# A fused attention and mixture kernel on one Trainium2 core: token copies, the first exponential, three operand splits and the read-back of g are placed anew

## The chip, the core and the metric

The kernel runs on one core of a Trainium2 chip. The core has five instruction streams that wait for one another by semaphores: TensorE (PE in the rows; its weight loads are PEld), VectorE (DVE), ScalarE (ACT), GpSimd (POOL) and SyncE (SP), which here issues every DMA. The metric is the device time of one execution in microseconds, median of several runs. The profile is of one further execution.

## What is computed

The reference, cut to what matters (the shapes are B=4, H=12, S=448, D=64; 1792 tokens of width 768; 8 experts of 4 slots, width 1024):

```python
scores = q @ k.T / sqrt(64) - log(448)          # per batch and head
x      = sigmoid(scores) @ v                    # -> (1792, 768)
g      = (x @ w_a) * (x @ w_b)                  # (1792, 1536)
x2     = g @ w_out                              # (1792, 768)
logits = x2 @ phi                               # (1792, 32)
d      = exp(logits - max over tokens); d /= sum over tokens
slot_in  = d.T @ x2                             # 32 slots
slot_out = relu(slot_in @ w1[e]) @ w2[e]        # 4 slots for each of 8 experts
c      = exp(logits - max over slots);  c /= sum over slots
out    = c @ slot_out
```

w_a, w_b and w_out come as 8-byte floats and are turned into 4-byte ones on the chip.

## The kernel before, in words

**Splits.** Most products are made of three matmuls: an operand t is kept as a rounded part (name with h) and a rest t - h (name with l), and hi x hi, hi x lo and lo x hi are summed in PSUM. So every operand costs one cast and one subtraction. `split_x`, `late_operands` and `block` make them; `late_operands` casts on ScalarE and subtracts on VectorE or GpSimd, by the name of the operand.

**Attention.** The 48 heads go in 24 pairs g. For a pair, `emit_TK` and `emit_TQ` transpose k and q through the two "ms" banks of PSUM, `emit_S` makes the scores of one of four chunks c and ScalarE turns each into a sigmoid (L185), `emit_PV` multiplies by v (16 matmuls, L195) and `emit_x` copies the result out of its "sc" bank (L218; L222 for batch 0). `att()` is a generator that yields after each piece. From pair 12 on (and before pair 6) a pair is "dense": its first chunk and the next pair's transposes stand ahead of the PV of the pair before it, then chunks 1, 2 and 3 follow. There are four "sc" banks, two "ab" banks (chunk 2 uses them in dense pairs) and two "ms" banks.

**The stages.** (1) Pairs 0 to 5. (2) `ab(0)`: g for batch 0, with pairs 6 to 11 woven in and w_a, w_b converted (`beats`) and written to DRAM as `ab32`. (3) The loop over `att_g` with pairs 12 to 23; beside it `operands()` makes sums of batches 1 and 2 on GpSimd, `prep_u(0)` the first weight blocks, and the first softmax step runs as a filler. (4) Twelve `unit(u)`s: batches 1 and 2 are multiplied together by a seven-product scheme; product m of a unit takes the operands ORDER = A11, S2, A12, S3, S1, A22, S4 (nine groups: three matmuls each of hi x hi, lo x hi, hi x lo) and one weight block `block(u, m)`, which is a cast on ScalarE and a subtraction on GpSimd (L574). T2, T3 and T4 are weight differences that VectorE makes from the raw tile `wr` (L583 to L589). Unit u+1's blocks are prepared during unit u by stepping `pu`, one step per product. S3, S1, A22 and S4 are the "late" operands, made at the start of unit 0, in memory that attention frees after its last PV. (5) `ab(3)`: g for batch 3; its weights come one half-product ahead from `ab32` (`load_w`, L425, the tiles `wr`), are cast on VectorE and subtracted on GpSimd (`split`, L433, L434). (6) `last_LG`, the slots, the experts' w1 and w2 from a ring of tiles (`pump`), and the output.

**Fillers.** `fill` is a list of generators; `fill_step` runs one step of the first. `group(b, gi)` turns four finished g tiles into tokens by transposes and copies (L486, L488). `LG(b)` makes the logits of batch b (matmul L716 into an "ms" bank `lf`), the maximum (VectorE), the exponential d and a copy of the logits (ScalarE, L733 and L738), transposes both (`tokens`, L752) and adds d.T @ g to `acc` (`dg`, L761). ScalarE has to load another function table ahead of the exponential and again ahead of the next sigmoid.

**g of batches 1 and 2.** Four token tiles are written to DRAM as `gk32` during the units and read back in `reload_gk` at i == 6 of `ab(3)` (i counts its yields, six to a column of weights) for LG(1) and LG(2). `pump` then loads one tile of `out32` or of an expert into each open slot, at every third i.

**What sets the order.** Each engine runs its instructions in the order in which the code emits them; an instruction waits only for semaphores. SP too is in order: a DMA that waits holds up all that are issued behind it, and nothing else makes SP keep pace with the loop that emitted it.

## Time and profile before

| what | us |
|---|---|
| median of 3 runs | 717.5 (716.67 to 718.07) |
| the profiled execution's own time | 717.61 |
| its span in the trace | 715.6 |
| mean granted TensorE clock | 0.984 of full |
| pairs 12 to 23 (stage 3) | about 215 to 311 |
| start of unit 0 up to unit 1 | 311 to 335 |
| units to the end | up to 485 |
| ab(3) | 485 to 600 |
| last softmax step | 600 to 623 |
| experts and output | 623 to 715.6 |

The stages are read from the timeline; 0 is the span's start. The execution's time is 2.0 us longer than the span, and 0.1 us longer than the median. In a timeline row the columns are start, length, engine, line, operation, output<-input, shape and count; the brackets give the idle time of that engine ahead of the row and what ended it. Lengths of neighbouring matmul rows overlap a little at their ends, so distances are taken from start to start. The granted clock is a share of full speed: 1.00 is 2.4 GHz and 0.50 is 1.2 GHz.

### The profile page before, as it was taken

The numbers are of one execution on the slowest core, as the hardware profiler recorded it, in microseconds if no ns is written. First come the engines' busy times: TensorE is split into PE (matmuls) and PEld (weight loads), VectorE is DVE, ScalarE is ACT, GpSimd is POOL, SyncE is SP. The second block draws the span as 40 slices with busy tenths as digits, with TensorE's granted clock in tenths as the row PEclk, the third lists the DMA queues.
The fourth block names the chain that finished last, engine by engine and source line by source line (L and its number), as shares of the span: only waits on it lengthen the run. The fifth ranks groups of instructions, "written<-read, shape, count | busy, mean of one in ns | idle before, by whom it ended". The sixth has DMA issues, their size and how long they took to land.

```text
span 715.6 us, 11048 instructions
## 1 busy us (share of the span) xinstructions
PE 663.9 (93%) x4187; PEld 476.7 (67%) x4187; DVE 358.9 (50%) x520; ACT 307.9 (43%) x557; POOL 303.2 (42%) x232
## 2 busy tenths in 40 slices
PE   6999999999999899998999999999979999997683
PEld 4557877776775454556998998898868896432131
DVE  4666899889735235226775567644323222300022
ACT  4887777878735577664233323311201011100021
POOL 0243677666634048009985665652333542100000
PEclk9999999999999999999999999999989999999998
DMA  8998999999724233201113411430997986999998
GB/s 200 254 295 207 287 310 302 271 300 283 227 84 136 72 81 76 70 2 46 38 53 80 147 52 45 118 140 23 259 352 277 367 307 229 359 416 415 410 352 270
DMA packets 104819, 146.90 MB, mean 205 GB/s; under 512 B 50880, under 2 KB 83904, under 8 KB 100800
## 3 DMA queue, kind: packets, MB, share of 16 engines
q1 hardware_dynamic: 104768, 146.22, 63.5%
q8 instruction: 33, 0.54, 0.3%
q14 instruction: 18, 0.15, 0.1%
HBM read 122.69 MB, written 23.50 MB: 204 GB/s over the span
## 4 chain that ended last, share of the span: by engine, by line
PE 77%; DMA 11%; DVE 4%; ACT 3%; POOL 2%; issue 1%; SPq 1%; ACTq 0%; DVEq 0%; POOLq 0%
PE ab L518 23%; PE sc L684 13%; PE sc L195 10%; DMA e<-in_moe_w 9%; PE sc L182 7%; PE ab L684 7%; PE ms L149 3%; PE ms L486 2%; DMA wr<-ab 2%; PE ab L182 1%; PE ms L468 1%; PE ms L761 1%; PE ms L377 1%; PE ms L364 1%; DVE gk L334 1%
## 5 line engine op out<-in xcount | busy, mean ns | idle before, releaser
L339 POOL TENSOR_TENSOR w<-gk,cy 128x768 int32<-128x768 int32 x36 | 66.2, 1839 | 91.6 <-DVE gk L334 60.1
L185 ACT ACTIVATE a<-sc,sums 112x448 f32<-112x448 f32 x158 | 89.2, 645 | 16.6 <-PE sc L182 16.5
L195 PE MATMUL sc<-a,vn 112*64 112x448 f32 x384 | 78.9, 552 | 2.7 <-ACT a L185 2.7
L518 PE MATMUL ab<-t,wh 128*128 128x448 f32 x288 | 66.0, 375 | 4.3 <-DVE wh L433 4.3
L434 POOL TENSOR_TENSOR wl<-wr,wh 128x768 fp32r<-128x768 f32 x22 | 40.5, 1840 | 68.1 <-DVE wh L433 39.6
L518 PEld LDWEIGHTS ab<-t,wh 128*128 128x128 f32 x288 | 54.0, 191 | 9.1 <-DVE wh L433 4.4
L195 PEld LDWEIGHTS sc<-a,vn 112*64 112x64 f32 x384 | 26.0, 138 | 41.9 <-issue 35.0
L525 ACT COPY misc<-ab 128x448 f32<-128x448 f32 x24 | 12.8, 534 | 77.0 <-PE ab L518 77.0
L434 POOL TENSOR_TENSOR wl<-w,wh 128x768 fp32r<-128x768 f32 x24 | 44.3, 1846 | 2.5 <-ACT wh L433 2.5
L1063 PE MATMUL ab<-e,gk 128*32 128x384 f32 x240 | 32.9, 521 | 12.4 <-DMA e<-in_moe_w 12.4
L332 DVE TENSOR_SCALAR mf<-gk 128x768 f32<-128x768 f32 x36 | 34.1, 946 | 13.8 <-ACT gk L321 13.6
L182 PE MATMUL sc<-qh,kh 64*112 64x448 f32 x158 | 36.6, 427 | 2.4 <-ACT a L185 1.0
L333 DVE TENSOR_SCALAR gk<-mf 128x768 uint32<-128x768 uint32 x36 | 34.3, 953 | 1.2
L518 PE MATMUL ab<-xh,wh 128*128 128x448 f32 x144 | 34.9, 377 | 0.0
L574 POOL TENSOR_TENSOR wx<-wr,wx 128x384 fp32r<-128x384 f32 x29 | 33.7, 1165 | 2.3 <-ACT wx L573 2.1
L518 PE MATMUL ab<-xl,wh 128*128 128x448 f32 x144 | 34.5, 375 | 0.0
L518 PE MATMUL ab<-xh,wl 128*128 128x448 f32 x144 | 34.5, 375 | 0.0
L518 PE MATMUL ab<-t,wl 128*128 128x448 f32 x144 | 34.0, 371 | 0.0
L1063 PEld LDWEIGHTS ab<-e,gk 128*32 128x32 f32 x240 | 9.6, 114 | 34.7 <-DMA e<-in_moe_w 23.9
L528 DVE TENSOR_TENSOR misc<-misc,ab 128x448 f32<-128x448 f32 x24 | 14.8, 616 | 35.0 <-PE ab L518 35.0
L574 POOL TENSOR_TENSOR wx<-T,wx 128x384 fp32r<-128x384 f32 x23 | 24.0, 1042 | 18.3 <-ACT wx L573 18.3
L573 ACT CAST wx<-T 128x384 fp32r<-128x384 f32 x23 | 11.8, 512 | 46.3 <-DVE T L589 30.9
(423 smaller groups left out, 1472.9 us busy)
## 6 DMA issues: line engine op xcount, KB each, us to landing
e<-in_moe_w SPq DMA_DIRECT2D x23, 1024.0 KB, 7.1
e<-in_moe_w SPq DMA_DIRECT2D x23, 768.0 KB, 15.1
wr<-ab SPq DMA_DIRECT2D x14, 768.0 KB, 4.9
ab<-w SPq DMA_DIRECT2D x24, 384.0 KB, 7.1
wr<-ab SPq DMA_DIRECT2D x18, 384.0 KB, 4.6
kn<-in_k SPq DMA_DIRECT2D x48, 112.0 KB, 4.7
qn<-in_q SPq DMA_DIRECT2D x48, 112.0 KB, 3.9
vn<-in_v SPq DMA_DIRECT2D x24, 224.0 KB, 3.9
```

What stands on the lines that cost most here:

```text
L149: pe.transpose(t[:, c * T:(c + 1) * T], a[:, c].rearrange("p h d -> p (h d)"), ident[:T, :T])
L182: pe.matmul(sc[h], kx[r, cs], qx[r], start=(i == 0), stop=(i == 2))
L185: act.activation(a, sc[h], AF.Sigmoid, bias=nlog[:T], scale=1.0 / math.sqrt(D))
L195: pe.matmul(pv_t[g][64 * h:64 * h + 64], qkv_t["v", g][:, h, c, :], a_t.pop((g, h, c)), start=(c == 0), stop=(c == C - 1))
L332: dve.tensor_scalar(mf, m, LOW, HIGH, op0=ALU.max, op1=ALU.min)
L333: dve.tensor_scalar(mi, mf.bitcast(U32), 3, 0x3FFFFFFF, op0=ALU.logical_shift_left, op1=ALU.bitwise_and)
L339: pool.tensor_tensor(thirds(w), m.bitcast(I32), thirds(cy_t.pop(x)), op=ALU.add)
L434: pool.tensor_tensor(wl, t, wh.bitcast(F32), op=ALU.subtract)
L518: pe.matmul(t, w[:, kk * 128:(kk + 1) * 128], xt[b * NP + kk][xi], start=(s == 0 and kk == 0), stop=(s == 2 and kk == KD - 1))
L574: pool.tensor_tensor(w[:, 1], t, w[:, 0].bitcast(F32), op=ALU.subtract)
L684: pe.matmul(t, w[:, wi, k * 128:(k + 1) * 128], xs[ORDER[m], k][xi], start=(s == 0 and k == 0), stop=(s == 2 and k == 2))
L1063: pe.matmul(sps[h][32 * j:32 * j + 32], hT[:, 2 * x + i, 2 * j + g], ring[order2[n + j]][0][:, i, c0:c0 + w], start=(g == 0 and x == 0 and ...
```

## The change

1. **Token copies.** `emit_x` copies out on VectorE for batches 2 and 3 (pairs 12 to 23) where ScalarE did; batch 1 stays on ScalarE with another form of copy.
2. **The first exponential.** `first_LG` takes the place of `group(0, 2)` and LG(0): the logits come before that group's transposes, the exponential is emitted right after a pair's last chunk of scores (`run["done"]`), and the group's four copies go to VectorE.
3. **Late operands.** VectorE subtracts for S3 and A22, GpSimd for S1 and S4 (before: VectorE S3 and S1, GpSimd A22 and S4). During unit 0 the steps of `prep_u(1)` go 0, 0, 0, 1, 2, 2, 2 to the seven products, where one went to each.
4. **Read-back.** `reload_gk(1)` at i == 6 and `reload_gk(2)` at i == 10; `pump` starts at i == 16 instead of i == 7.

```diff
--- before.py
+++ after.py
@@ -215,7 +215,7 @@
         b, kk = divmod(g, NP)
         if b:
             xt[g] = raw_x(b, kk)
-            act.activation(xt[g], pv, AF.Copy)
+            (act.copy if b == 1 else dve.tensor_copy)(xt[g], pv)
         else:
             xh = x0p.tile([128, S], F32R, tag=f"xh{kk}", name=f"xh{kk}")
             xl = x0p.tile([128, S], F32R, tag=f"xl{kk}", name=f"xl{kk}")
@@ -263,6 +263,7 @@
                     yield 430
                 for c in range(len(first), C):
                     emit_S(g, (c,))
+                    run["done"] = c == C - 1
                     yield 800
 
     PAIR = 860 + 4 * 800 + 3200
@@ -478,7 +479,7 @@
             gk = gk_01[:, gi] if gi < 2 else gk_2
         gkt = gk[:T]
         gk = gk[:T].rearrange("p (c n) -> p c n", c=C)
-        if (b, gi) == (B - 1, 2):
+        if gi == 2 and b in (0, B - 1):
             yield
         for c in range(C):
             tp = ms((T, 512))
@@ -497,13 +498,12 @@
             sp.dma_start(out=gk32[b - 1, gi], in_=gkt)
         gtok[b, gi] = gk
 
-    def reload_gk():
-        for b in (1, 2):
-            for gi in range(2):
-                nm = f"e1{2 * b + gi}"
-                t = run["e1"].tile([128, 2048], F32, tag=nm, name=nm)[:T]
-                sp.dma_start(out=t, in_=gk32[b - 1, gi])
-                gtok[b, gi] = t.rearrange("p (c n) -> p c n", c=C)
+    def reload_gk(b):
+        for gi in range(2):
+            nm = f"e1{2 * b + gi}"
+            t = run["e1"].tile([128, 2048], F32, tag=nm, name=nm)[:T]
+            sp.dma_start(out=t, in_=gk32[b - 1, gi])
+            gtok[b, gi] = t.rearrange("p (c n) -> p c n", c=C)
 
     def ab(b):
         for fc in range(KF):
@@ -527,7 +527,9 @@
                             g = gT_all[n % 5]
                             dve.tensor_tensor(g, g, t, op=ALU.mult)
                             gT[b, fc] = g
-                            if fc % 4 == 3 and (b, fc) != (B - 1, KF - 1):
+                            if (b, fc) == (0, KF - 1):
+                                fill.append(first_LG())
+                            elif fc % 4 == 3 and (b, fc) != (B - 1, KF - 1):
                                 fill.append(group(b, fc // 4))
                     next(pr, None)
                     yield (fc * 12 + i * 6 + s * 2 + 2) / (KF * 12)
@@ -622,7 +624,7 @@
     def late_operands(nm):
         n = {"S3": NP, "S1": 2 * NP, "A22": 2 * NP + 3, "S4": NP + 3}[nm]
         for i in range(3):
-            split_x(nm, i, xt[n + i], pools["xb"], (f"{nm}h{i}", f"{nm}l{i}"), act.copy, dve if nm in ("S3", "S1") else pool)
+            split_x(nm, i, xt[n + i], pools["xb"], (f"{nm}h{i}", f"{nm}l{i}"), act.copy, dve if nm in ("S3", "A22") else pool)
 
     def last_x():
 
@@ -728,6 +730,8 @@
             dve.tensor_tensor(dm, m0, mx, op=ALU.subtract)
         run["m"] = mx
         yield
+        while not b and not run.pop("done", False):
+            yield
         sm = col()
         ls, d = run["lsd"]
         act.activation(d, lf, AF.Exp, bias=nm, accum_out=sm)
@@ -737,8 +741,6 @@
             run["al"] = al
         act.copy(ls, lf)
         yield
-        if not b:
-            yield
         if b:
             sn = col()
             dve.scalar_tensor_tensor(sn, run["s"], al, sm, op0=ALU.mult, op1=ALU.add)
@@ -788,6 +790,18 @@
         elif b == B - 2:
             run.pop("lsd2")
             open_slots(run["e1"], [1, 4, 5])
+
+    def first_LG():
+        gr, lg = group(0, 2, (dve.tensor_copy,) * 4), LG(0)
+        for _ in range(GDEL + 1):
+            next(gr)
+            yield
+        while "s" not in run:
+            next(lg)
+            yield
+        yield from gr
+        yield
+        yield from lg
 
     def last_LG():
 
@@ -926,13 +940,13 @@
     x0_ctx.close()
     pools["cp"] = cp_ctx.enter_context(tc.tile_pool(name="cp", bufs=1, side="left"))
     run["lsd2"] = pools["cp"].tile([128, 2 * S + 2 * C * NS], F32, name="ls_d")
-    fill.append(LG(0))
     ops, pu = operands(), None
     load_u(0)
     load_u(1)
     for cost in att_g:
         if not run.pop("trans", False):
             fill_step()
+        run.pop("done", None)
         if next(ops, 0) == 0:
             pu = pu or prep_u(0)
             next(pu, None)
@@ -960,7 +974,8 @@
                 next(lx, None)
             if u + 1 == NU and m in (1, 3):
                 split(NU * 3, w_raw.pop(LAST + m // 2), dve.tensor_copy)
-            next(pu, None)
+            for _ in range((0, 0, 0, 1, 2, 2, 2)[m] if u == 0 else 1):
+                next(pu, None)
             fill_step()
     run["banks"] = 1
     load_w(LAST + 4)
@@ -980,13 +995,15 @@
             run["wr"] = e1.tile([128, 2048], F32, tag="e10", name="wr")
             load_w(LAST + 6)
             load_w(LAST + 7)
-            reload_gk()
+            reload_gk(1)
             open_slots(e1, range(6, NE1))
             fill.append(LG(1))
             fill.append(LG(2))
+        elif i == 10:
+            reload_gk(2)
         elif i == 12:
             open_slots(gkp, [0])
-        if i > 6 and i % 3 == 1:
+        if i > 14 and i % 3 == 1:
             pump()
     for kk in range(NP):
         xt.pop((B - 1) * NP + kk)
```

How it moves instructions. **ScalarE at the first exponential**, before (r is the x tile of pairs 12 to 14, a the sigmoids, ls_d the exponential and the logits of batch 0):

```order
L218 ACTIVATE r_2608<-sc 128x448
L185 ACTIVATE a<-sc,sums 112x448 x2
L185 ACTIVATE a<-ab,sums 112x448 x2
L185 ACTIVATE a<-sc,sums 112x448 x4
L218 ACTIVATE r_2703<-sc 128x448
L733 ACT_TABLE_LOAD
L733 ACTIVATE ls_d,sums<-ms,sums 128x448
L738 COPY ls_d<-ms 128x448
L185 ACT_TABLE_LOAD
L185 ACTIVATE a<-sc,sums 112x448 x2
```

ScalarE at the same place, now:

```order
L185 ACTIVATE a<-sc,sums 112x448 x10
L185 ACTIVATE a<-ab,sums 112x448 x2
L185 ACTIVATE a<-sc,sums 112x448 x2
L737 ACT_TABLE_LOAD
L737 ACTIVATE ls_d,sums<-ms,sums 128x448
L742 COPY ls_d<-ms 128x448
L185 ACT_TABLE_LOAD
L185 ACTIVATE a<-sc,sums 112x448 x4
L185 ACTIVATE a<-ab,sums 112x448 x2
```

The exponential stood behind an x copy, ahead of chunks 1, 2 and 3 of a pair whose chunk 0 was done; now it stands behind chunk 3 of pair 12 and ahead of chunk 0 of pair 13, and there are no x copies in the row.

**TensorE there, now** (L718 is the logits matmul, kn and qn the transposes of k and q, L195 the PV, L487 the group's transposes):

```order
L718 MATMUL ms<-misc,selF 128x448
L149 MATMUL ms<-ident,qn 128x112 x4
L195 MATMUL sc<-a,vn 64x448 x8
L182 MATMUL sc<-qh,kh 112x448 x2
L182 MATMUL sc<-qh,kl 112x448 x2
L182 MATMUL sc<-ql,kh 112x448 x2
L182 MATMUL ab<-qh,kh 112x448 x2
```

and, after chunk 3 of pair 12, up to chunk 1 of pair 13:

```order
L149 MATMUL ms<-ident,kn 128x112 x4
L182 MATMUL sc<-qh,kh 112x448 x2
L182 MATMUL sc<-qh,kl 112x448 x2
L182 MATMUL sc<-ql,kh 112x448 x2
L149 MATMUL ms<-ident,qn 128x112 x4
L195 MATMUL sc<-a,vn 64x448 x8
L487 MATMUL ms<-ident,misc 112x128 x4
L182 MATMUL sc<-qh,kh 112x448 x2
```

Between the logits and the first instruction that needs the exponential's bank or its sigmoids there are now two PVs and the chunks of a pair.

**GpSimd at the late operands**, before and then now (S4l, A22l, S1l are rests of late operands, the names with wx, wl, wh rests of unit 1's weight blocks, in the order of its products):

```order
L574 TENSOR_TENSOR wl_3618<-wr,wl_3618 128x384
L596 TENSOR_TENSOR A22l_3636<-gk_93,A22h_3635 128x448
L596 TENSOR_TENSOR A22l_3640<-gk_93,A22h_3639 128x448
L596 TENSOR_TENSOR A22l_3644<-gk_93,A22h_3643 128x448
L574 TENSOR_TENSOR wx_3647<-T_3615,wx_3647 128x384
L596 TENSOR_TENSOR S4l_3662<-t_1803,S4h_3661 128x448
```

```order
L598 TENSOR_TENSOR S1l_3604<-r_2592,S1h_3603 128x448
L598 TENSOR_TENSOR S1l_3608<-r_2681,S1h_3607 128x448
L598 TENSOR_TENSOR S1l_3612<-r_2790,S1h_3611 128x448
L598 TENSOR_TENSOR S4l_3650<-t_1803,S4h_3649 128x448
L598 TENSOR_TENSOR S4l_3654<-t_2096,S4h_3653 128x448
L598 TENSOR_TENSOR S4l_3658<-t_2425,S4h_3657 128x448
L576 TENSOR_TENSOR wl_3675<-wr,wl_3675 128x384
L576 TENSOR_TENSOR wx_3693<-T_3672,wx_3693 128x384
```

The two blocks that stood among the late operands now stand behind all of them, and S1l has changed places with A22l.

**VectorE there, now** (T is T3, then T2; wr the raw weights; gk_94 the running sums of unit 0's products):

```order
L598 TENSOR_TENSOR S3l_3600<-t_1531,S3h_3599 128x448
L693 TENSOR_TENSOR gk_94<-sc,gk_94 128x448
L598 TENSOR_TENSOR A22l_3627<-gk_93,A22h_3626 128x448
L598 TENSOR_TENSOR A22l_3631<-gk_93,A22h_3630 128x448
L598 TENSOR_TENSOR A22l_3635<-gk_93,A22h_3634 128x448
L676 TENSOR_TENSOR misc<-sc,gk_94 128x448
L698 TENSOR_TENSOR gk_94<-ab,gk_94 128x448
L585 TENSOR_TENSOR T_3673<-wr 128x384
L586 TENSOR_TENSOR wr<-wr 128x384
L587 TENSOR_TENSOR T_3672<-wr 128x384
```

T3 and T2 of unit 1 stood ahead of the sums of products 1 to 3; now they stand behind A22l and those sums.

**SP in ab(3)**, before and then now (wr is a weight load, e<-gk the read-back, e<-out the first pumped tiles, clog a store of logits):

```order
L425 DMA wr<-ab_99 128x768 x2
L505 DMA e_5230<-gk_102 112x2048
L505 DMA e_5232<-gk_102 112x2048
L505 DMA e_5234<-gk_102 112x2048
L505 DMA e_5236<-gk_102 112x2048
L881 DMA e_5244<-out_100 128x4x512
L881 DMA e_5279<-out_100 128x4x512
L773 DMA clog_101<-lsd_5226 448x1x32
L881 DMA e_5319<-out_100 128x4x512
L425 DMA wr<-ab_99 128x768
```

```order
L426 DMA wr<-ab_99 128x768 x2
L505 DMA e_5230<-gk_102 112x2048
L505 DMA e_5232<-gk_102 112x2048
L505 DMA e_5273<-gk_102 112x2048
L505 DMA e_5275<-gk_102 112x2048
L775 DMA clog_101<-lsd_5226 448x1x32
L426 DMA wr<-ab_99 128x768
L895 DMA e_5340<-out_100 128x4x512
L426 DMA wr<-ab_99 128x768
L895 DMA e_5419<-out_100 128x4x512
```

The four read-backs stand where they stood, one behind the other; the third weight load had three pumped tiles ahead of it and now has none.

## Rows read from the trace of the kernel before

**Rows 1.** The page: the chain that ended last, shares of the span by engine.

```profile
PE 77%; DMA 11%; DVE 4%; ACT 3%; POOL 2%; issue 1%; SPq 1%; ACTq 0%; DVEq 0%; POOLq 0%
```

**Rows 2.** Stretches: length, busy time (count) PE, PEld, DVE, ACT, POOL; clock, DMA, GB/s.

```profile
530.00:533.00 3.00, 2.03 (x5) 1.82 (x6) 1.62 (x5) 0.00 (x0) 1.83 (x1) 0.50 1.07 366
590.00:595.00 5.00, 5.00 (x26) 4.63 (x26) 1.65 (x3) 0.00 (x0) 2.68 (x2) 1.00 0.23 76
623.00:716.00 93.00, 66.54 (x504) 25.33 (x496) 11.24 (x22) 9.93 (x22) 0.00 (x0) 0.95 0.98 372
```

**Rows 3.** Timeline of TensorE around the first exponential, and a pair without one.

```profile
238.34 0.40 PE L752 MATMUL ms<-ident,ls_d 32*112 32x32 f32 x4 [1.11 <-ACT ls_d L738]
...
240.28 0.98 PE L182 MATMUL sc<-qh,kh 64*112 64x448 f32 x2 [1.01 <-ACT a L185]
...
242.90 4.37 PE L195 MATMUL sc<-a,vn 112*64 112x448 f32 x16
...
252.48 0.46 PE L182 MATMUL sc<-qh,kh 64*112 64x448 f32 x2
...
253.81 3.23 PE L195 MATMUL sc<-a,vn 112*64 112x448 f32 x16
```

**Rows 4.** Timeline of ScalarE around the first exponential, and a pair without one.

```profile
235.84 1.28 ACT L733 ACT_TABLE_LOAD   x1
...
239.59 1.16 ACT L185 ACTIVATE a<-sc,sums 112x448 f32<-112x448 f32 x2
...
260.01 2.22 ACT L185 ACTIVATE a<-sc,sums 112x448 f32<-112x448 f32 x4
...
264.98 1.16 ACT L185 ACTIVATE a<-sc,sums 112x448 f32<-112x448 f32 x2 [0.27 <-PE sc L182]
```

**Rows 5.** Timeline of TensorE from unit 0's second product to unit 2.

```profile
316.27 0.88 PE L684 MATMUL sc<-S2h,wx 128*128 128x448 f32 x3
...
325.96 0.47 PE L684 MATMUL sc<-A22l,wl 128*128 128x448 f32 x1 [0.94 <-POOL A22l L596]
...
334.85 0.77 PE L684 MATMUL sc<-S2h,wx 128*128 128x448 f32 x3
...
356.20 0.78 PE L684 MATMUL sc<-A22h,wx 128*128 128x448 f32 x3
```

**Rows 6.** Timeline of GpSimd at the late operands and in unit 2.

```profile
321.59 4.32 POOL L596 TENSOR_TENSOR A22l<-gk,A22h 128x448 fp32r<-128x448 f32 x3
...
351.86 1.34 POOL L574 TENSOR_TENSOR wx<-T,wx 128x384 fp32r<-128x384 f32 x1
```

**Rows 7.** Timeline of VectorE at the late operands.

```profile
317.44 1.70 DVE L596 TENSOR_TENSOR S3l<-t,S3h 128x448 fp32r<-128x448 f32 x3 [17.71 <-ACT S3h L595]
...
320.66 1.38 DVE L583 TENSOR_TENSOR T<-wr 128x384 f32<-128x384 f32 x1
...
327.15 0.61 DVE L699 TENSOR_TENSOR gk<-sc,gk 128x448 f32<-128x448 f32 x1
```

**Rows 8.** Timeline of TensorE in ab(3).

```profile
513.51 1.96 PE L761 MATMUL ms<-e,lsd 112*32 112x128 f32 x64
...
521.99 2.59 PE L518 MATMUL ab<-t,wh 128*128 128x448 f32 x12
...
530.97 2.61 PE L518 MATMUL ab<-t,wh 128*128 128x448 f32 x6 [4.31 <-DVE wh L433]
533.51 2.84 PE L761 MATMUL ms<-e,lsd 112*32 112x128 f32 x64
```

**Rows 9.** Timeline of GpSimd in ab(3).

```profile
511.23 1.85 POOL L434 TENSOR_TENSOR wl<-wr,wh 128x768 fp32r<-128x768 f32 x1 [1.40 <-PE ab L518]
```

**Rows 10.** The chain that ended last in ab(3): start, us, what.

```profile
510.60 4.27 SPq L773
...
517.99 12.24 DMA wr<-ab
```

**Rows 11.** DMA rate, 485 to 600 in 40 slices of 2.875 us.

```profile
GB/s 6 130 0 0 6 14 365 268 262 254 259 250 363 376 395 368 308 334 379 322 328 185 31 388 348 358 342 394 409 344 387 414 284 306 362 272 154 7 31 311
```

## Prediction

> **What bounds the kernel now.** I read the chain of waits first, then the idle times of TensorE in the timeline, then the table by stretches. Of the chain that ended last 77% is TensorE's and 11% DMA's [rows 1]. The DMA part is nearly all at the end: from 623 to 716 the engines of the DMA are 0.98 busy at 372 GB/s [rows 2], and loads of the experts set the pace. Up to 600 TensorE sets it, so an edit there is worth what it takes from TensorE's idle time, and from the half-speed clock that comes behind an idle time. Three places show both. At the first exponential TensorE waits 1.11 us for ScalarE's copy and 1.01 us for a sigmoid, and the PV behind it takes 4.37 us where it takes 3.23 in another pair [rows 3]. At the late operands it waits for GpSimd [rows 5]. In ab(3) it waits 4.31 us for a cast [rows 8], and the chain behind that ends in a weight load that took 12.24 us [rows 10]; from 530 to 533 the clock is 0.50, which is 1.2 GHz [rows 2]. The change touches these three places and nothing else of weight.
>
> Whether a gain ahead of 600 reaches the end depends on the loads of the experts. They wait for open slots, not for bytes: from 590 to 595 the DMA is 0.23 busy with 76 GB/s [rows 2], and the slices from 588 to 597 fall to 154, 7 and 31 GB/s [rows 11]. So the last 93 us should come forward with TensorE, one for one, as long as this hole isn't filled.
>
> **First exponential.** Removed: the waits of 1.11 and 1.01, then 4.37 - 3.23 = 1.14 of slow PV, and the slow matmuls ahead of it: from the restart of the scores to the PV 242.90 - 240.28 = 2.62 us, in the other pair 253.81 - 252.48 = 1.33 [rows 3]. Of these 1.29 I count 0.9 as clock, since about 0.4 is another transpose that stands there. Together 1.11 + 1.01 + 1.14 + 0.9 = 4.16. Added: the same ScalarE work at another place. It takes 239.59 - 235.84 = 3.75 us from the first table load to the next sigmoids. The hole on ScalarE between two pairs is 264.98 - 262.23 = 2.75, where the four sigmoids that begin at 260.01 end at 262.23 [rows 4]. So the next pair's first sigmoids come 1.0 late. What hides that 1.0 is TensorE's own work: behind the scores of chunk 0 it still has transposes, a PV of 3.23 and the group's transposes before it needs the bank or those sigmoids. I take 0.1 of wait, at most 0.7, which is the wait for one sigmoid. Gain 4.16 - 0.1, rounded 4.1. Bounds: 2.5 (0.7 of wait and the 0.9 not clock) and 4.2 (nothing late).
>
> The Trainium skill, "ScalarE: Activation LUTs", section What ACT_TABLE_LOAD costs, gives some 1.28 us for the load and 1.38 more for a drain behind it. The row has 1.28 for the load, and load, exponential, copy and second load fit into 3.75 together, so no such drain shows. By the page the chain would be 3.75 + 2 x 1.38 = 6.5, an estimate, some 3.8 over the hole; a gain of about 1.5 rather than 4.1. The row decides.
>
> **Token copies.** Pairs 12 to 23 lose an x copy on ScalarE, which lies in its hole, and VectorE gets one. The nearest row is VectorE's sum of a bank into the running sums, 0.61 for the same 128x448 [rows 7], taken while GpSimd was busy with S4l. TensorE wants the bank back a chunk or more after the PV. I take 0, with 0.5 to either side over all twelve pairs; if VectorE were busy with something else at each PV's end, the cost is rival 4.
>
> **Late operands.** A product lasts (356.20 - 334.85) / 11.67 = 1.83 us, from unit 1's second product to the third trio of unit 2's sixth, which is eleven and two thirds products on [rows 5]. Seven products should take 12.8 us; from unit 0's second to unit 1's second they take 334.85 - 316.27 = 18.58. So 5.75 are lost there, as waits for the rests of A22 and S4 and as slow clock behind them. The cause is GpSimd's queue: A22l takes 4.32 for three [rows 6] (1.44 each), S4l stands behind it, and weight rests of unit 1 stand in between.
>
> Now: S3h on ScalarE as before, S3l on VectorE 0.56 each (1.70 for three [rows 7]), S1l on GpSimd from about 318.4, S4l behind it to about 326.2, at 1.2 to 1.44 each. A22l on VectorE runs beside S1l. Alone VectorE needs 0.56 for such a subtraction, but T took 1.38 while GpSimd had A22l [rows 7, 6], so I give 1.4 each: about 319.8 to 324.1. TensorE wants A22l from 324.29 on and S4l from 327.5 on, so both are just in time; 0.2 for S1l. Next is T2 of unit 1, which stands behind these on VectorE: two sums of 0.61, T3, the raw sum and T2 itself, ready near 328.3, wanted at 316.27 + 12.83 = 329.1. Then GpSimd: unit 2's sixth block had its rest finished at 351.86 + 1.34 = 353.2 [rows 6], and TensorE used it at 356.20 [rows 5], 3.0 of slack. TensorE now comes 5.55 earlier, GpSimd only about 1.1 (between 0.3 and 1.9, by how long it idles for T2). So 5.55 - 1.1 - 3.0, about 1.4, comes back as a stall in unit 2. Gain 5.75 - 0.2 - 1.4 = 4.15. Bounds: 2.5 (GpSimd hardly earlier, T2 a little late) and 5.75 (nothing late).
>
> The Trainium skill, "SBUF — State Buffer", section Who interferes with whom, speaks against this edit: a VectorE instruction with two SBUF inputs contends with a GpSimd instruction that reads SBUF, so A22l should not run beside S1l at its own 0.56. The rows bear it out in T's 1.38. Without it the late operands would gain about 5.5 instead of 4.15.
>
> **Read-back and pump.** The split itself changes nothing that SP sees: nothing waits between the two parts, so the four read-backs still go one behind the other. What moves is the pump. The third weight load of ab(3) was issued at 517.99 and took 12.24 us [rows 10], since SP stood in the store of logits until 510.60 + 4.27 = 514.87 and two pumped tiles were ahead of the load in the queues. Now it waits only for its slot, until GpSimd's rest ends at 511.23 + 1.85 = 513.08 [rows 9]. Ahead of it are four read-backs of 0.92 MB and two weight loads of 0.39, 4.46 MB; by 513.1 about 3.1 MB of them are there, by the slices from 502 on at 365, 268, 262 and 254 GB/s [rows 11]. So 1.35 + 0.39 = 1.7 MB at 260 GB/s remain, 6.6 us: it lands near 520. TensorE wanted the cast at 530.97 - 4.31 = 526.7. The wait goes, and with it the half-speed clock: six matmuls in 2.61 where twelve take 2.59, 1.3 us, and L761's 2.84 against 1.96, 0.88 [rows 8]. Gain 4.31 + 1.3 + 0.88 = 6.5. Bounds: 2 (the load late by 4.5) and 6.5.
>
> The price is the experts' loads: three tiles of 1.05 MB are pumped nine steps later, 3.15 MB at 372 GB/s, some 8.4 us of DMA. The hole at 588 to 597 has 3 x 2.875 us at 372 less what flowed, 2.66 MB, and 0.29 more in the slice ahead: 2.95 MB [rows 11]. They fit almost exactly, so I count 0 and keep the 8.1 that the last loads could be late by as a rival.
>
> **The sum.** 4.1 + 0 + 4.15 + 6.5 = 14.75, rounded with the 0.1 by which the profiled execution (717.61, span 715.6) lies over the median: 717.61 - 14.75 = 702.86, less 0.1 to stand on the median, 702.8. The parts lie one behind the other in time and on the same engine, so they add.
>
> **Rivals.** 1. GpSimd and VectorE take back most at the units: GpSimd no earlier (stall 5.55 - 3.0 = 2.55) and T2 1.5 late; 5.75 - 0.2 - 2.55 - 1.5 = 1.5 is kept of 4.15, so 705.5. For it: both queues carry as much as before. Against: nothing but T2 holds GpSimd. 2. The weight load is late all the same, because the burst of read-backs ahead of it is the same 3.67 MB; all 6.5 stay lost, 709.3. Against: 6 us between 520 and 526. 3. The tail doesn't come forward: the three late tiles meet a full DMA and push the experts by 8.1, 710.9. Against: the hole in the slices; for: it only just fits. 4. Slower: VectorE's token copies come late in each pair, behind its running sums and weight differences, and TensorE waits for the bank. It costs more than the other parts gain once a pair loses 14.75 / 12 = 1.2 us; at 1.5 in each, 12 x 1.5 = 18, 720.8. Against: 0.61 for such an instruction even beside GpSimd, and little else on VectorE in these pairs. 5. More: the late operands lose nothing and the clock gains further, 5.75 and some waits of the pairs, below 700.5.
>
> **How the numbers follow.** Forecast 0.62 (700.5 to 705), rival 1 0.12, rival 2 0.08, rival 3 0.08, rival 4 0.06, rival 5 0.04. The predicted time is the forecast's, 702.8. From 700 to 709.5 the range holds forecast, rivals 1 and 2 and a part of 5, about 0.83; 3 and 4 are left out. About 0.2%, 1.4 us, is what a measurement of this kernel can tell from no change. Faster: all but rival 4 and mixtures of the late cases, 0.92; slower 0.05; within it 0.03.
>
> **What would show it.** First exponential: the idle times ahead of TensorE's transposes of the exponential and of the next scores gone, PV near 3.23. Late operands: unit 1's second product 12.8 to 13.5 behind unit 0's, no wait for A22l or S4l, A22l near 1.4 each on VectorE, and a wait of about 1.4 in unit 2 for a weight rest. Read-back: the third weight load lands before 526, no clock of 0.50 there, no idle time for the cast. Tail: still about 93 us long, and the slices ahead of it without a hole. The prediction is wrong if the tail is longer, if TensorE waits for x copies, or if the stall in unit 2 is over 3 us.

## The result, and the profile after

The changed kernel takes 704.79 us (median of 4 runs, 704.48 to 705.82), the kernel before 717.57 beside it: a ratio of 0.983 (0.981 to 0.984). 702.8 was forecast, in a range of 700.0 to 709.5. The profiled execution took 704.98 us with a span of 703.2. So 12.4 us left the span, where 14.75 had been summed.

Where they left is read from TensorE's timeline, as distances between seven of its rows. The columns are start, length, engine, line, operation, output<-input, shape and count, and in brackets the idle time ahead and what ended it. After:

```profile
206.28 3.23 PE L195 MATMUL sc<-a,vn 112*64 112x448 f32 x16
...
312.26 0.87 PE L686 MATMUL sc<-S2h,wx 128*128 128x448 f32 x3
...
325.82 0.78 PE L686 MATMUL sc<-S2h,wx 128*128 128x448 f32 x3
...
353.73 0.78 PE L686 MATMUL sc<-S2h,wx 128*128 128x448 f32 x3
...
454.71 0.77 PE L686 MATMUL sc<-S2h,wx 128*128 128x448 f32 x3
...
589.40 1.02 PE L718 MATMUL ms<-misc,selF 128*128 128x448 f32 x2 [0.71 <-DVE misc L473]
...
678.47 0.91 PE L1108 MATMUL ms<-gk,selF 128*128 128x384 f32 x2 [0.62 <-ACT gk L1106]
```

They are the last PV ahead of the loop over pairs 12 to 23, the second product of units 0, 1, 3 and 10, the last softmax step, and the first product behind the experts. In the kernel before, the same rows begin at 205.74, 316.27, 334.85 (the last two in [rows 5]), 360.50, 461.48, 602.56 and 690.34.

| stretch | before, us | after, us | gain | forecast |
|---|---|---|---|---|
| start to that PV | 205.74 | 206.28 | -0.54 | 0 |
| PV to unit 0 (first exponential) | 110.53 | 105.98 | 4.55 | 4.1 |
| unit 0 to unit 1 (late operands) | 18.58 | 13.56 | 5.02 | 5.55 |
| unit 1 to unit 3 | 25.65 | 27.91 | -2.26 | -1.4 |
| unit 3 to unit 10 | 100.98 | 100.98 | 0 | 0 |
| unit 10 to the last softmax step (ab(3)) | 141.08 | 134.69 | 6.39 | 6.5 |
| there to the end of the experts' products | 87.78 | 89.07 | -1.29 | 0 |
| there to the end | 25.26 | 24.73 | 0.53 | 0 |

The gains add to 12.40. The last stretch but one, 87.78 us before and 89.07 after, is called the tail below. These distances are a better measure than the total. Over the experiments the first stretch came out between 204.3 and 206.3 us, though of the edits only `undo_copies` touches it (the form of batch 1's copy), while the stretches in the middle, where nothing in them was changed, repeat within 0.1, that of ab(3) within 0.35 and the two about the late operands within 0.5.

**First exponential.** On ScalarE the exponential now has chunk 3's sigmoids ahead of it and takes 3.76 us from its table load to the next sigmoids, as in [rows 4]:

```profile
228.00 1.18 ACT L185 ACTIVATE a<-sc,sums 112x448 f32<-112x448 f32 x2
229.19 1.28 ACT L737 ACT_TABLE_LOAD   x1
230.49 0.63 ACT L737 ACTIVATE ls_d<-ms,sums 128x448 f32<-128x448 f32 x1
...
232.95 1.16 ACT L185 ACTIVATE a<-sc,sums 112x448 f32<-112x448 f32 x2
```

On TensorE a PV runs beneath it, and neither the next PV nor the transposes of the exponential wait, where [rows 3] had 1.11 and 1.01 of idle time and a PV of 4.37:

```profile
229.49 3.23 PE L195 MATMUL sc<-a,vn 112*64 112x448 f32 x16
...
239.38 3.23 PE L195 MATMUL sc<-a,vn 112*64 112x448 f32 x16
...
243.34 0.40 PE L754 MATMUL ms<-ident,ls_d 32*112 32x32 f32 x4
```

**Late operands.** Of the waits in [rows 5] one of 0.37 us for S4l is left, and a new one of 1.71 stands in unit 2, for a weight rest from GpSimd:

```profile
323.06 0.47 PE L686 MATMUL ab<-S4l,wh 128*128 128x448 f32 x1 [0.37 <-POOL S4l L598]
...
349.33 0.88 PE L686 MATMUL sc<-A22h,wx 128*128 128x448 f32 x3 [1.71 <-POOL wx L576]
```

**Weight load.** The third weight load of ab(3) is issued at 506.33 (SP), VectorE waits 1.80 us for it, and TensorE comes to its cast at 519.82 without waiting. The clock from 518 to 521 is 1.00, where [rows 2] had 0.50:

```profile
506.33 0.34 SPq L426 DMA_DIRECT2D wr<-ab  x1
```

```profile
516.22 0.56 DVE L434 CAST wh<-wr 128x768 fp32r<-128x768 f32 x1 [1.80 <-DMA wr<-ab]
```

```profile
518.00:521.00 3.00, 3.00 (x19) 2.42 (x17) 1.58 (x4) 0.00 (x0) 0.74 (x1) 1.00 0.89 293
```

### The profile page after: what moved, and what is told of

It reads as the page before. It is cut to its first block, busy times and chain, and to the rows that moved or that the text cites. A ratio compares the mean times of both kernels' runs of the same rounds, so it can differ in the third digit from the quotient of the medians.

```text
span 703.2 us, 11039 instructions
## 1 busy us (share of the span) xinstructions
PE 659.2 (94%) x4187; PEld 472.9 (67%) x4187; DVE 373.7 (53%) x534; ACT 301.0 (43%) x543; POOL 306.1 (44%) x232
## 4 chain that ended last, share of the span: by engine, by line
PE 75%; DMA 12%; DVE 6%; ACT 2%; POOL 2%; issue 1%; SPq 0%; ACTq 0%; POOLq 0%
PE ab L518 21%; PE sc L686 13%; PE sc L195 10%; DMA e<-in_moe_w 9%; PE sc L182 7%; PE ab L686 7%; PE ms L149 3%; PE ms L487 2%; DMA ab<-w 2%; DVE gk L335 2%; PE ab L182 1%; PE ms L763 1%; PE ms L469 1%; DVE gk L334 1%; DVE mf L333 1%
## 5 line engine op out<-in xcount | busy, mean ns | idle before, releaser
L195 PE MATMUL sc<-a,vn 112*64 112x448 f32 x384 | 77.8, 546 | 2.1 <-ACT a L185 2.1
L195 PEld LDWEIGHTS sc<-a,vn 112*64 112x64 f32 x384 | 25.7, 136 | 40.3 <-issue 34.0
L1080 PE MATMUL ab<-e,gk 128*32 128x384 f32 x240 | 34.6, 540 | 13.0 <-DMA e<-in_moe_w 12.9
```

What stands on the lines that cost most here:

```text
L195: pe.matmul(pv_t[g][64 * h:64 * h + 64], qkv_t["v", g][:, h, c, :], a_t.pop((g, h, c)), start=(c == 0), stop=(c == C - 1))
L1080: pe.matmul(sps[h][32 * j:32 * j + 32], hT[:, 2 * x + i, 2 * j + g], ring[order2[n + j]][0][:, i, c0:c0 + w], start=(g == 0 and x == 0 and ...
```

## The experiments

### Which edit freed the first exponential

Two kernels each undo one of the two edits that touch it. Without the new place (`undo_exp`; `first_LG` and the wait for `run["done"]` are gone):

```diff
-                            if (b, fc) == (0, KF - 1):
-                                fill.append(first_LG())
...
-        while not b and not run.pop("done", False):
-            yield
...
+    fill.append(LG(0))
     ops, pu = operands(), None
```

> The changed kernel with only the placing of the first exponential as before (the group's transposes, then the logits, then the exponential wherever the filler comes to it); token copies, late operands and the pump stay changed. Theory: the parts add, and this one is worth what the traces show up to unit 0, 4.0 us: 708.8 us (708 to 709.5), with TensorE again idle by 1 us or more ahead of the transposes of the exponential or of the next scores. Rival: the token copies on VectorE had already emptied ScalarE enough, so the old place costs little: 705 to 706. Rival: what is lost here is made up in the units, where the late rests set the pace anyway: 706 to 707.

Measured: 703.89 us, ratio 0.979 (0.976 to 0.982). The stretch from the PV to unit 0 took 106.37, against 105.98 with the edit and 110.53 in the kernel before. So the theory fell: nearly all of that stretch's gain, 4.16 us of 4.55, was there without the edit. The timelines of ScalarE tell why. Before, an x copy that waits for the PV stands ahead of the table load:

```profile
235.28 0.54 ACT L218 ACTIVATE r<-sc 128x448 f32<-128x448 f32 x1 [3.18 <-PE sc L195]
235.84 1.28 ACT L733 ACT_TABLE_LOAD   x1
```

In `undo_exp`, with that copy on VectorE, the table load follows the sigmoids of chunk 0 and is over by the time the PV, which begins at 231.47 (TensorE), has ended:

```profile
230.42 1.16 ACT L185 ACTIVATE a<-sc,sums 112x448 f32<-112x448 f32 x2 [0.52 <-PE sc L182]
231.65 1.28 ACT L732 ACT_TABLE_LOAD   x1
```

```profile
231.47 3.23 PE L195 MATMUL sc<-a,vn 112*64 112x448 f32 x16
```

The other half, the copies alone undone (`undo_copies`):

```diff
-            (act.copy if b == 1 else dve.tensor_copy)(xt[g], pv)
+            act.activation(xt[g], pv, AF.Copy)
```

> The changed kernel with the token copies of batches 1 to 3 on ScalarE as before; the new place of the first exponential stays. The run without the new place lost nothing, since ScalarE, without the x copy that waits for the PV, came to the exponential under the PV. Theory: either of the two edits takes the wait away, and this one too stays where it is: 704.8 us (704 to 705.5), no idle time ahead of the transposes of the exponential. Rival: only the copies matter, and with them back 4.0 are lost: 708.8. Rival (the prediction's own sum): the copies are worth 0, within 0.5; this rival and the theory differ in what the run without the new place has shown, not here.

Measured: 704.17 us, ratio 0.979 (0.977 to 0.982); the unaltered kernel on the same chip 703.07. The stretch took 106.28. Either edit alone brings about 4.2 us of the 4.55, and the second adds 0.3 to 0.4: they are two ways to take the x copy from ahead of the exponential, and their gains don't add.

### The late operands

`undo_late` undoes both parts, `old_engines` and `old_steps` one each:

```diff
-            split_x(nm, i, xt[n + i], pools["xb"], (f"{nm}h{i}", f"{nm}l{i}"), act.copy, dve if nm in ("S3", "A22") else pool)
+            split_x(nm, i, xt[n + i], pools["xb"], (f"{nm}h{i}", f"{nm}l{i}"), act.copy, dve if nm in ("S3", "S1") else pool)
```

```diff
-            for _ in range((0, 0, 0, 1, 2, 2, 2)[m] if u == 0 else 1):
-                next(pu, None)
+            next(pu, None)
```

> The changed kernel with the late operands as before: A22 subtracted on GpSimd and S1 on VectorE, and one step of the next unit's blocks to each product of unit 0. Theory: the traces give 5.0 us at unit 0 of which 2.2 come back as a stall in unit 2, so this is worth 2.8: 707.6 us (707 to 708.3), unit 0's second product to unit 1's second about 18.6 us, no stall in unit 2. By the prediction it was worth 4.15: 708.9. Rival: the stall in unit 2 has nothing to do with the new order (GpSimd would be late there in any case once TensorE comes earlier), then it stays and the loss is about 5: 709.8.

Measured: 708.06 us, ratio 0.985 (0.981 to 0.989); 18.33 from unit 0 to unit 1 and 25.71 on to unit 3, 44.04 in sum, against 41.47 with the change, and 41.5 to 41.9 in the other runs that keep it. The edit is worth 2.1 to 2.6 us, and the stall in unit 2 belongs to it. Much of the rest of this run's loss of time is a tail of 90.32, of which more below.

> The changed kernel with only the steps as before, one of the next unit's blocks to each product of unit 0; S1 on GpSimd and A22 on VectorE as changed. Theory (steps are most of the gain): T3 and T2 stand ahead of A22l on VectorE and two blocks between the late rests on GpSimd, so TensorE waits for A22l or S4l: 16 to 18.5 us from unit 0's second product to unit 1's (13.56 unaltered), and less stall in unit 2 (26 to 27 instead of 27.91): 1.5 to 3 us slower in sum. Rival (the swap of engines is the gain): 13.5 to 14.5.

Measured: 705.03 us, ratio 0.981 (0.979 to 0.984); 17.24 and 25.72, 42.96 in sum, 1.1 to 1.5 more than with the steps late, and 1.1 less than with neither edit (44.04). T3 and T2 stand ahead of A22l again, on VectorE now, and TensorE waits for A22l:

```profile
321.31 0.48 PE L686 MATMUL sc<-A22l,wl 128*128 128x448 f32 x1 [0.87 <-DVE A22l L598]
322.78 0.47 PE L686 MATMUL sc<-A22l,wl 128*128 128x448 f32 x1 [1.00 <-DVE A22l L598]
```

> The changed kernel with only the engines of the late operands as before: A22 on GpSimd, S1 on VectorE; the steps of the next unit's blocks stay late (0, 0, 0, 1, 2, 2, 2). Distances in the trace are the measure, since the total differs by some 2 us between executions in stages that the change doesn't touch. Unaltered: 13.56 us from unit 0's second product to unit 1's, 27.91 from there to unit 3's. Both edits undone: 18.33 and 25.71. Theory: most of the gain is the steps, which put the late operands' rests ahead of the blocks on GpSimd; GpSimd still subtracts six late operands, and A22l, which TensorE wants later than S1l, comes first or in time: 13.6 to 15, then 27 to 28, some 0 to 1 us slower than the unaltered kernel. Rival: the swap of engines is the gain, and without it the first distance is 17 to 18.5.

Measured: 702.82 us, ratio 0.978 (0.975 to 0.981), against 705.03 for `old_steps` on the same chip. Its profiled execution took 3548.55 us, so there are no distances, only the time of the other three. It is not slower than the two measurements of the unaltered kernel (0.983 and 0.978), and faster than `old_steps`: most of the gain is that the blocks of unit 1 wait until the late operands are done. With the steps as before, the swap of engines alone was worth 44.04 - 42.96 = 1.1 us; whether it adds anything once the steps are late stays open.

### What stalls unit 2

`relief` takes two multiplications of unit 1 from GpSimd, `later_x` takes the operands of batch 3 (L638) out of unit 1:

```diff
-                put((1, f1), 0, t, tm["p1"], tm["p1"], pool)
+                put((1, f1), 0, t, tm["p1"], tm["p1"], dve if u == 1 else pool)
...
-                put((2, f1), 2, t, tm["u3"], tm["u3"], pool)
+                put((2, f1), 2, t, tm["u3"], tm["u3"], dve if u == 1 else pool)
```

> The changed kernel, but in unit 1 the two multiplications of a finished pair of tokens' g (two of 1.15 and 1.47 us on GpSimd) go to VectorE. Theory: TensorE's 1.71 us of idle time in unit 2 is GpSimd's queue, which stands at the same time behind unit 0 as before while TensorE comes 5.0 earlier; with 2.6 us taken from it ahead of the late rest, the stall goes, and 2.0 to 2.2 us are gained: 702.7 us against the unaltered one's 704.8. Rival: the rest is late because VectorE's T4 and the cast behind it are late, then nothing is gained, or VectorE with two more subtractions ahead is later: 704.8 to 706. Rival: the stall moves on to the next block of unit 2 with half its size: 703.8.

Measured: 702.19 us, ratio 0.976 (0.974 to 0.979), the unaltered kernel on the same chip 703.07. Unit 1 to unit 3 took 26.45 instead of 27.92, so 1.47 of the 2.27 are gone. What is left is a wait of 0.49:

```profile
346.54 0.88 PE L686 MATMUL sc<-A22h,wx 128*128 128x448 f32 x3 [0.49 <-POOL wx L576]
```

GpSimd lost part of the relief beside VectorE's new work: the subtractions of L638, 1.16 to 1.48 us each in unit 1 of the changed kernel, took 1.47 to 1.55 each, this one for instance:

```profile
335.68 1.54 POOL L638 TENSOR_TENSOR t<-t,t 128x448 fp32r<-128x448 f32 x1
```

```diff
-            elif u >= 1:
+            elif u >= 2 and m % 2:
                 next(lx, None)
```

> The changed kernel, but batch 3's operands (a cast on ScalarE and a subtraction on GpSimd of 1.15 to 1.47 us each, six of them), which ab(3) needs only some 130 us later, are made in units 2 and 3, at every second product, and not in unit 1. Moving two multiplications to VectorE took 1.46 of the 2.26 us that unit 2's stall costs; VectorE then slowed the other subtractions on GpSimd (1.53 instead of 1.15). Theory: GpSimd's queue is the stall; with 7 to 8 us less in it, none remains and the distance from unit 1's second product to unit 3's is 25.65 as in the kernel before: 2.2 us faster than the unaltered one, about 701 us. Rival: the rest waits for VectorE's T4 and its cast: 27 or more. Rival: units 2 and 3 get a stall of their own from the moved work, 0.5 to 2 us.

Measured: 701.62 us, ratio 0.977 (0.974 to 0.980). Unit 0 to unit 1 took 13.25, unit 1 to unit 3 25.75, and 100.99 on to unit 10: no stall in unit 2, and none where the work went. So GpSimd's queue was the stall. The rival, T4 and its cast, is ruled out by the changed kernel's own trace. The rest that TensorE waits for in unit 2 is that of the sixth block, which is made of T4. ScalarE had cast it by 339.21, nine us before GpSimd came to its rest:

```profile
338.70 0.51 ACT L575 CAST wx<-T 128x384 fp32r<-128x384 f32 x1 [2.38 <-DVE T L591]
```

```profile
348.28 1.00 POOL L576 TENSOR_TENSOR wx<-T,wx 128x384 fp32r<-128x384 f32 x1
```

### The read-back, the pump and the tail

```diff
-        if i > 14 and i % 3 == 1:
+        if i > 6 and i % 3 == 1:
```

> The changed kernel with the pump beginning where it began before (i == 7), the read-back still in two parts. Theory: the place of the pump is the whole of the read-back edit's gain; the third weight load is late again with TensorE idle for some 4 us and a clock of 0.50 behind it, 6.4 lost there, and the tail gets back the 0.8 to 1.3 us that the late tiles cost it: 709.9 to 710.4 us. Rival: the read-back in two parts already lets the weight load through: 704 to 706.

Measured: 712.01 us, ratio 0.991 (0.989 to 0.994). The load is late again and the stretch to the last softmax step takes 142.57, 7.9 more than with the change and 1.5 more than in the kernel before (on SP a pumped tile now stands between the two parts of the read-back; no run shows whether that is the 1.5):

```profile
524.97 2.61 PE L518 MATMUL ab<-t,wh 128*128 128x448 f32 x6 [5.45 <-DVE wh L434]
```

> The changed kernel with both parts of the read-back issued together at i == 6 as before, the pump beginning at i == 16. Theory: the split changes nothing that SP sees, the four read-backs go one behind the other either way, so the same as the unaltered one within 0.3 us: 704.8. Rival: the second part now comes a little later or behind a weight load, and without the split the third weight load is late by a us or more: 706 to 711.

Here `reload_gk(2)` follows `reload_gk(1)` at i == 6. Measured: 702.98 us, ratio 0.978 (0.975 to 0.980), the unaltered kernel on the same chip 703.07; the stretch took 134.76, as there. The pump's place is the whole gain, the read-back in two parts none of it.

For `pump13` the bound in that line is i > 11.

> The changed kernel with the pump beginning one turn earlier (i == 13 instead of i == 16): one tile of 1.05 MB, 2.7 us of DMA, goes ahead of the third weight load, and every later tile is one turn earlier. That load landed at 516.1 in the changed kernel and TensorE used it at 519.8. Theory: it still lands in time (518.8, then 0.6 of cast), and the tail gets its 0.8 to 1.3 us back since one tile less is pushed behind 585: 703.5 to 704.1 us. Rival: the load is late by a us or two and its cost in idle time and clock outweighs it: 706 to 708. Rival: the loss in the tail has nothing to do with the displaced tiles: 704.8.

Measured: 703.29 us, ratio 0.979 (0.975 to 0.981). The cast of the third weight load came at 517.97, 1.8 us later than in the changed kernel; TensorE didn't wait for it (134.76). The tail took 87.58 against 89.07. The hole ahead of the last softmax step is read from the last 17 us before it, in the table by stretches (busy times of the five engines, then clock, DMA share and GB/s): before, after, and `pump13`:

```profile
585.56:602.56 17.00, 16.29 (x80) 13.44 (x79) 3.98 (x7) 1.07 (x2) 5.53 (x3) 1.00 0.48 155
```

```profile
572.40:589.40 17.00, 16.29 (x80) 13.44 (x79) 4.17 (x7) 1.07 (x2) 5.54 (x3) 1.00 0.95 345
```

```profile
572.33:589.33 17.00, 16.29 (x81) 13.44 (x79) 4.17 (x7) 1.07 (x2) 5.54 (x3) 1.00 0.82 279
```

With the three displaced tiles the hole is filled to 0.95; with one tile less displaced, 0.18 stays free.

> The changed kernel itself, unaltered, as the measure for the others of this chip. 704.8 us is expected (704 to 705.5). In the first profile the first product with the slots' outputs came 89.07 us behind the last softmax step's start, against 87.78 in the kernel before. If the displaced tiles fill the hole only just, this distance stands near 88 to 89 and differs between executions; if it is fixed by the order, it is 89.07 again.

Measured: 703.07 us, ratio 0.978 (0.976 to 0.981), with a tail of 87.71. So the 89.07 was not fixed by the order. Where the pump begins at 16, nine profiled executions of this kernel and its variants had 87.5 to 87.8 six times, and 89.07, 89.10 and 90.32 in the others; where it begins earlier, all four had 87.5 to 87.8 (the kernel before, `pump7`, `pump13` and the run below). That fits a hole that is filled only just, but three against none is no proof, and two readings speak against it. The same 17 us were filled to 0.93 in `after_again`, with a tail of 87.71, and to 0.93 in `undo_late`, with 90.32. And some 7 us into the last softmax step DMA nearly comes to a halt in the execution with 89.07 (33 GB/s) as in `after_again` (0), so what had been pushed late seems to have landed there by then; only `undo_late` still moved 401. In this order, the changed kernel, `after_again` and `undo_late`:

```profile
596.40:597.40 1.00, 0.26 (x6) 0.23 (x3) 0.84 (x3) 0.00 (x0) 0.96 (x2) 1.00 0.08 33
```

```profile
594.51:595.51 1.00, 0.26 (x6) 0.23 (x3) 0.84 (x3) 0.00 (x0) 0.97 (x2) 1.00 0.00 0
```

```profile
598.21:599.21 1.00, 0.26 (x6) 0.24 (x3) 0.84 (x3) 0.00 (x0) 0.96 (x2) 1.00 0.95 401
```

So what makes a tail long stays open.

> The one before, and the pump begins at i == 13 instead of i == 16. The distance from the last softmax step's start to the first product with the slots' outputs was 89.07, 87.71, 87.67 and 87.51 us where the pump begins at 16, 87.58 and 87.78 where it begins at 13 and at 7. Theory: 16 lies at the edge, where the hole is filled in some executions and not in others, so an earlier pump takes the 1.4 us of the bad ones away and nothing of the good ones: 87.6 here, some 0 to 1 us faster than the one before in the median, about 700.5 us. Rival: the distance has nothing to do with the pump and shows 89 here in one of the runs too: the same as the one before.

Measured: 700.99 us (700.11 to 701.30), ratio 0.975 (0.973 to 0.978), with a tail of 87.54. It has the lowest time of all. Against `later_x` on the same chip, 701.62 (700.75 to 703.56), the difference lies within the spread.

## Why the prediction was right, and where its steps were not

**The total** was 2 us too low, within the range (0.3 by the second measurement of the same kernel, 703.07). In the first execution's distances two terms came out smaller than counted, the two of the late operands, and one had been counted at nothing, the tail; the first stretch took 0.54 more with nothing forecast for it.

**First exponential: right in size, the copies' part wrong.** 4.1 was forecast, 4.55 came, and the new place alone does bring 4.25, as its working has it (`undo_copies`). But the working gave 0, within 0.5, to the token copies, and they alone bring 4.16 (`undo_exp`). That the sum came out right all the same is luck of the order in which it counted: behind the new place the copies add only 0.3, within their 0.5, and counted first they would be 4.16 and the new place 0.4. The step that failed is "pairs 12 to 23 lose an x copy on ScalarE, which lies in its hole". The copy is short and the hole is there, but the copy waits for the PV, and whatever stands behind it on ScalarE waits too. In eleven pairs that is nothing urgent (all twelve copies back cost 0.3 us in `undo_copies`); in one it was the exponential. The row that says so is the bracket of 3.18 at 235.28, and the prediction had begun its reading one row too late, at the table load. That the two edits overlap was not among the rivals. The clock's 0.9 was too much as well. The two rows that stood 2.62 us apart in the kernel before stand 2.18 apart in `undo_exp`, without a wait and at a clock of 1.00 from 237 to 240, so 0.44 at most was the clock's:

```profile
237.54 0.98 PE L182 MATMUL sc<-qh,kh 64*112 64x448 f32 x2
...
239.72 3.23 PE L195 MATMUL sc<-a,vn 112*64 112x448 f32 x16
```

The drain of some 1.38 us that the Trainium skill adds to a table load ("ScalarE: Activation LUTs", section What ACT_TABLE_LOAD costs) doesn't show here either. The sigmoids of 228.00 and 1.18 end at 229.18, the load of 229.19 and 1.28 ends at 230.47, and the exponential begins at 230.49, so there is no room for it on either side.

**Late operands: the mechanism right, two terms mis-sized.** Unit 1 was forecast 5.55 us earlier and came 5.02 earlier, since S4l was not quite in time. GpSimd took 4.55 for S4l's three, 1.52 each where 1.2 to 1.44 had been given, and A22l on VectorE took 4.61, 1.54 each where 1.4 had been given. The working also had TensorE come to S4l at 327.5, a time read from the kernel before, behind its wait for A22l. With that wait gone TensorE came to S4l at 322.12, 9.86 behind unit 0's second product, which is 326.1 in those times. And the T of 1.38, from which the 1.4 was taken, ran mostly beside a weight rest (320.23, below) and not beside A22l; the next T, beside A22l, took 1.40, so nothing hangs on it. The changed kernel:

```profile
314.50 4.00 POOL L598 TENSOR_TENSOR S1l<-r,S1h 128x448 fp32r<-128x448 f32 x3 [32.30 <-ACT S1h L597]
318.45 4.55 POOL L598 TENSOR_TENSOR S4l<-t,S4h 128x448 fp32r<-128x448 f32 x3
...
325.33 1.03 POOL L576 TENSOR_TENSOR wx<-T,wx 128x384 fp32r<-128x384 f32 x1 [1.04 <-ACT wx L575]
...
332.14 1.48 POOL L638 TENSOR_TENSOR t<-t,t 128x448 fp32r<-128x448 f32 x1
```

```profile
315.86 4.61 DVE L598 TENSOR_TENSOR A22l<-gk,A22h 128x448 fp32r<-128x448 f32 x3 [0.46 <-ACT A22h L597]
```

The stall in unit 2 was forecast with place and cause, at 1.4; it cost 2.26. The term that failed is "GpSimd only about 1.1" earlier. Behind unit 0's second product, GpSimd came to L638 at 332.14 - 312.26 = 19.88 us; before, that subtraction (L636 there) began at 336.13, 336.13 - 316.27 = 19.86:

```profile
320.23 1.40 POOL L574 TENSOR_TENSOR wl<-wr,wl 128x384 fp32r<-128x384 f32 x1 [34.05 <-ACT wl L573]
...
326.84 3.66 POOL L596 TENSOR_TENSOR S4l<-t,S4h 128x448 fp32r<-128x448 f32 x3
...
336.13 1.27 POOL L636 TENSOR_TENSOR t<-t,t 128x448 fp32r<-128x448 f32 x1 [0.17 <-ACT t L635]
```

GpSimd starts 1.7 us sooner (2.24 behind that product, 3.96 before) and loses that again to the 1.04 in which it waits for T2's cast and to the slower S4l (4.55 where it took 3.66). By the prediction's own formula, 5.02 - 0 - 3.0 gives 2.0, close to what was measured. `later_x` and the early cast of T4 show the queue to be the cause.

**Read-back and pump: right.** 6.5 was forecast, 6.39 came, and `one_readback` and `pump7` bear out both sentences, that the split does nothing and the pump's place does all. The load's landing was too early in the forecast: 6.6 us from its issue, measured 9.9 up to the cast that waits for it. So 3.0 us were to spare (519.82 less 0.6 of cast, less 516.22), not 6. And three pumped tiles had stood ahead of the load on SP before, where the working names two.

**The tail: the rival that fits "almost exactly".** It was counted at 0 and kept as a rival with 8.1 for all three tiles; a longer tail was on the prediction's list of what would show it wrong. What came is 1.29 more in one execution and 0.07 less in another of the same kernel, so the rival's 8.1 didn't come. The tiles had been summed to exceed the hole by 0.2 MB, 0.5 us at 372 GB/s. A hole overrun by a little is the price in between that the working left out, but no run shows that the 1.29 is that price.

## What to carry to other kernels

An instruction that waits has the price of all that stands behind it on its engine, not its own length: look at the bracket of the row ahead of the late one, and remove whichever of the two is cheaper to move. When one engine is sped up, ask of every queue that feeds it whether it comes earlier by as much; what doesn't becomes the next stall, and its size is the difference less the slack. Edits that free the same wait are counted once, and stretches between fixed rows show a gain of half a us where the total of an execution varies by two.

## What the runs showed of the hardware

VectorE and GpSimd slowed each other: three subtractions with both operands in SBUF took 4.61 us on VectorE (A22l) beside S1l at 4.00 and the first half of S4l at 4.55 on GpSimd, where VectorE took 1.70 for three with GpSimd idle (S3l in [rows 7]). Two multiplications moved from GpSimd to VectorE brought the six subtractions of L638 on GpSimd from 1.31 us in the mean to 1.52. And two executions of the changed kernel differ by 2.0 us in the first stretch and by 1.4 in the tail, with the stretches in between the same to 0.1.
